# Infini-attention block with feed-forward: q and k projected as 32-column tiles straight from the raw weights, heads regrouped, new order of work

## The chip, the core and the metric

The kernel runs on one core of a Trainium2 chip. The metric is the device time of one execution in microseconds (us), lower is better. A time is given as the median of several runs; beside it there is one execution recorded by the hardware profiler, with its own time and its span (first to last recorded instruction).

The core has four computing engines that run side by side, each with its own instruction queue in program order: TensorE (PE; its weight loads are listed apart as PEld), VectorE (DVE), ScalarE (ACT) and GpSimd (POOL). SyncE (SP) issues the DMA transfers. Engines wait for each other on semaphores. All matmuls write to PSUM, which has 8 banks of 2 KB per partition; SBUF holds everything else.

## The reference, cut to what matters

One batch of 2048 tokens with 640 features, 32 heads of 20, bf16. The attention works on 4 segments of 512 tokens: causal softmax inside the segment, plus a compressive memory of all segments before.

```python
qs, ks, vs = q[:, :, s], k[:, :, s], v[:, :, s]          # from layernorm(x) @ wq, wk, wv
p = softmax(qs @ ks^T * scale + causal_mask)
a_dot = p @ vs
a_mem = (phi(qs) @ M) / (phi(qs) @ z + 1e-6)             # phi(t) = t + 1 if t > 0 else exp(t)
o = g * a_mem + (1 - g) * a_dot                          # g = sigmoid(beta), one per head
M = M + phi(ks)^T @ vs;  z = z + sum(phi(ks))            # carried to the next segment
...
h  = x + concat_heads(o) @ wo
h2 = h + silu(layernorm(h) @ w1) @ w2                    # 640 -> 1728 -> 640
```

## The kernel before, in words

**Layout.** The work of each segment is cut into 5 *chunks* of projected features (128 rows each) for q and for k, 8 *groups* of 4 heads, and 4 token blocks of 128. A group of heads sits in one tile of 128 partitions, one head in the first 20 rows of each quarter of 32 rows. Five such tiles (`QK`, `QK0` for segment 0) come straight from the projections and hold heads 0 to 19; the 12 rows that are free in each quarter carry pieces of heads 20 to 31 along. From these pieces 12 DMAs per segment (`virt`, line 897) put together the tiles `QKV` of groups 5 to 7.

**Weights of q and k.** The raw weights `wraw` lie, after their DMAs, in the room that `sT` has later. Since a chunk's 128 columns are not next to each other in them, `rearr` (lines 689 to 721) copies them into `wqr` and `wkr`: 12 tasks (`re_wq0`, `re_wq0h`, `re_wq1` to `re_wq4`, and the same for k), spread over VectorE, ScalarE and GpSimd by the order.

**A segment's front.** Layer norm of each block (`n1_st` statistics, `n1_rs` 1/sqrt on GpSimd, `n1_ap` apply); transposes to `tT` (in segment 0 five matmuls with the identity, `n1_tp`, and an eviction from PSUM, `n1_te`; in the others a DMA, `n1_tr`); projections `pr{s}{c}{w}` (w = 0 for q, 1 for k; five matmuls of 512 columns in two parts, `.0` and `.1`), evicted by `qe` (line 866 on ScalarE, 867 on VectorE); values `v` and their eviction `ve` (lines 832 and 833, into `Vx`, for segment 0 into a part of `sT`); phi by `ex` (exponential on ScalarE, line 873), `pa` and `pb` (VectorE). Chunk 0 of segment 0 is projected in halves of 256 tokens (`SPLIT0`, x and y).

**A group of heads** k = 8 s + g. Scores in quads of four row tiles, one head each (`qk{k}a`, `b`, `e`, matmuls at line 943 with `tile_position=(32*r, 0)`); exponentials `e{k}...` over two PSUM banks at once (line 964, 128x1024) or, where the order marks it `/W`, over four (line 960, 128x2048); causal masks `mk` on GpSimd; the product with V as four column tiles (`av`, line 999); its eviction times a gate (`oe`); then, back to tokens, `td` and from segment 1 on the memory part `tm`; normalisation `nm` on VectorE and `ad` on GpSimd. At a segment's end `kt`, `mz`, `ma`, `mb` update the memory, masked by `MzM`, which GpSimd makes at the start from the masks `mt`. The back of a segment is `ot`, `wo`, `rs`, `n2_...`, `h1` (matmuls), `th` (Tanh), `s`, `h2`, `o`, `out`.

**Forms of a matmul.** `mms` (line 547) emits either one matmul over the full array (line 550) or, where the order marks a task `/C`, four column tiles of 32 columns (line 551):

```python
    def mms(eng, out, lhsT, rhs, start, stop):

        if eng != "cols":
            return [lambda e: e.matmul(out, lhsT=lhsT, rhs=rhs, start=start, stop=stop)]
        return [lambda e, p=p: e.matmul(out[p:p + 32, :], lhsT=lhsT[:, p:p + 32], rhs=rhs, start=start, stop=stop,
                                        tile_position=(0, p)) for p in (0, 32, 64, 96)]
```

**What sets the order.** A table, `ORDER`, written out as text: 1439 entries in one sequence for all engines, each a task with, where there is a choice, its engine (`/A` ScalarE, `/D` VectorE, `/G` GpSimd, `/C` column tiles) and the slots of its buffers. `Graph.schedule` follows it and checks that predecessors come first; `Tracker` then adds the semaphore waits from what is read and written. So each engine's queue is fixed by the table. Entries `fillN` are N matmuls of 256 columns on a tile of zeros, `zpad` (line 622); nothing uses their result. There are 25 of them before the first transposes and 5 behind these. `zpad` is set to zero by VectorE (line 601), before the statistics of block 0. `warm` is a Tanh on ScalarE that reads `zpad` and writes two rows of `w2_sb`.

**Loads.** SyncE issues x blocks 0 and 1, blocks 2 and 3 together, wq and wk in two parts each, wv; the later loads (x4 on, wo, w1, w2) wait for the rearrangement of wk's first part.

## Time and profile before

| | |
|---|---|
| median of 3 runs | 296.78 us (296.61 to 297.32) |
| the profiled execution | 297.21 us, span 295.2 us |
| TensorE busy | 280.6 us (95%) |
| VectorE busy | 219.0 us (74%) |
| ScalarE busy | 216.5 us (73%) |
| GpSimd busy | 148.2 us (50%) |
| granted TensorE clock, mean | 1.0 |

A row of a timeline or chain gives start, length, engine, what is written, the line, and a count (x5) where several instructions are taken together; `out<-in` are the names of the tiles. A matmul's shape is contraction*output rows, then contraction x columns streamed. Matmuls are pipelined, so that one's listed length is longer than the time until the next one can start: durations here are taken from start to start of a run of many. A page's share of busy time is a mean over stages with different limits; the stages are read by stretches of the span.

### The profile page before, as it was taken

What the parts mean: (1) busy time and instruction counts of PE and PEld (TensorE: products, weight loads), DVE (VectorE), ACT (ScalarE), POOL (GpSimd) and SP (SyncE); (2) the same over time, 40 slices, a digit from 0 to 9 for tenths busy, and PEclk for the clock granted to TensorE, in tenths of its full rate; (3) what the DMA queues carried; (4) which work ended last, traced back from release to release, by engine and by line L of the source; (5) the groups of instructions that cost most, each with busy time, mean ns of one, the idle gap of its engine ahead of it and who ended that gap; (6) DMA issues with size and microseconds to landing.
All of it is one profiled execution on the core that took longest, in us unless ns stands there. A gap on an engine that the chain in (4) does not pass through costs nothing.

```text
span 295.2 us, 8471 instructions
## 1 busy us (share of the span) xinstructions
PE 280.6 (95%) x3537; PEld 158.1 (54%) x3561; DVE 219.0 (74%) x447; ACT 216.5 (73%) x263; POOL 148.2 (50%) x297
## 2 busy tenths in 40 slices
PE   7899889899999999999999999999999999999996
PEld 5554434536644545566643564556564657764574
DVE  4788899689999677999879867597655676734614
ACT  5799999799989999957899856979989641004500
POOL 4878777662777436946527552548464621300000
PEclk9999999999999999999999999999999999999999
DMA  7859349476530400442553312303221031330003
GB/s 223 288 151 232 57 115 229 96 235 90 87 66 18 104 4 3 75 100 46 81 135 101 77 27 53 58 2 54 62 69 47 2 67 26 67 91 0 0 2 111
DMA packets 48597, 24.72 MB, mean 84 GB/s; under 512 B 38896, under 2 KB 47472, under 8 KB 48560
## 3 DMA queue, kind: packets, MB, share of 16 engines
q1 hardware_dynamic: 48560, 24.19, 34.9%
q8 instruction: 28, 0.46, 0.6%
q14 instruction: 9, 0.07, 0.1%
HBM read 10.41 MB, written 2.62 MB: 44 GB/s over the span
## 4 chain that ended last, share of the span: by engine, by line
PE 64%; ACT 17%; DVE 10%; issue 3%; DMA 2%; POOL 2%; ACTq 0%; DVEq 0%
PE ps_all L550 47%; ACT PT L964 12%; PE ps_all L551 7%; PE ps_all L943 5%; PE ps_all L999 4%; DVE stt L754 3%; ACT PT L960 2%; DVE xn_rot L772 2%; DVE sT L1222 2%; DMA tT<-otok 2%; ACT th L1216 1%; ACT ex L873 1%; POOL PT L976 1%; DVE x_tok L1181 1%; PE ps_all L1117 1%
## 5 line engine op out<-in xcount | busy, mean ns | idle before, releaser
L964 ACT ACTIVATE PT<-ps_all 128x1024 bf16<-128x1024 f32 x114 | 109.3, 1035 | 15.5 <-PE ps_all L943 14.8
L976 POOL TENSOR_SCALAR_AFFINE_SELECT PT<-PT 128x512 bf16<-128x512 bf16 x128 | 82.0, 649 | 57.5 <-ACT PT L964 32.0
L1216 ACT ACTIVATE th<-ps_all 128x512 f32<-128x512 f32 (+1 forms) x56 | 31.5, 585 | 36.6 <-PE ps_all L550 27.8
L550 PE MATMUL ps_all<-w_sb,sT 128*128 128x320 bf16 x400 | 58.2, 299 | 0.1
L550 PE MATMUL ps_all<-tT,w_sb 128*128 128x512 bf16 x225 | 53.9, 379 | 1.3 <-issue 1.1
L1222 DVE SCALAR_TENSOR_TENSOR sT<-th,ps_all 128x512 bf16<-128x512 f32 (+1 forms) x56 | 36.2, 663 | 17.7 <-ACT th L1216 17.1
L550 PEld LDWEIGHTS ps_all<-w_sb,sT 128*128 128x128 bf16 x400 | 38.1, 98 | 16.6 <-issue 1.5
L960 ACT ACTIVATE PT<-ps_all 128x2048 bf16<-128x2048 f32 x23 | 43.2, 1879 | 3.4 <-PE ps_all L943 3.0
L550 PEld LDWEIGHTS ps_all<-tT,w_sb 128*128 128x128 bf16 x235 | 21.4, 98 | 25.0 <-issue 1.8
L754 DVE BATCH_NORM_STATS2 stt<-x_tok 128x6 f32<-128x320 bf16 x62 | 26.8, 473 | 1.3 <-DMA x_tok<-in_A_x_dram 1.2
L1259 DVE SCALAR_TENSOR_TENSOR x_tok<-ps_all,x_tok 128x640 bf16<-128x640 f32 (+1 forms) x17 | 13.2, 784 | 18.0 <-PE ps_all L550 17.1
L1077 POOL TENSOR_TENSOR otok<-on 128x320 bf16<-128x320 bf16 x24 | 19.2, 806 | 12.5 <-DVE on L1069 12.5
L867 DVE CAST QK<-ps_all 128x512 bf16<-128x512 f32 x26 | 17.9, 687 | 8.0 <-PE ps_all L550 6.5
L764 POOL TENSOR_TENSOR rst<-mvt,eps_c 128x1 f32<-128x1 f32 x32 | 7.0, 219 | 31.9 <-DVE mvt L757 30.0
L550 PE MATMUL ps_all<-tT,wkr 128*128 128x512 bf16 (+1 forms) x87 | 21.7, 368 | 1.0 <-issue 0.5
L772 DVE TENSOR_SCALAR xn_rot<-x_tok,mvt,rst 128x640 bf16<-128x640 bf16 x32 | 17.8, 564 | 4.3 <-POOL rst L766 3.8
L550 PE MATMUL ps_all<-tT,wqr 128*128 128x512 bf16 (+1 forms) x79 | 20.0, 367 | 1.0 <-issue 0.6
L1069 DVE TENSOR_TENSOR on<-ps_all,rd 128x640 bf16<-128x640 f32 x24 | 19.8, 824 | 0.8
L550 PE MATMUL ps_all<-wv_sb,tT 128*128 128x320 bf16 x130 | 19.7, 299 | 0.7 <-issue 0.7
L766 POOL TENSOR_TENSOR rst<-rst,eps_c 128x1 f32<-128x1 f32 x32 | 18.0, 563 | 2.5
L1015 DVE TENSOR_SCALAR oTs<-ps_all,lsc 128x512 bf16<-128x512 f32 x24 | 17.8, 742 | 0.8 <-PE ps_all L999 0.8
L999 PE MATMUL ps_all<-PT,Vx 128*32 128x512 bf16 (+3 forms) x384 | 17.3, 301 | 0.0
(113 smaller groups left out, 379.5 us busy)
## 6 DMA issues: line engine op xcount, KB each, us to landing
out_dram<-x_tok SPq DMA_DIRECT2D x15, 160.0 KB, 1.9
w_sb<-in_B_w_dram SPq DMA_DIRECT2D x5, 432.0 KB, 4.7
x_tok<-in_A_x_dram SPq DMA_DIRECT2D x3, 640.0 KB, 4.3
w_sb<-in_B_w_dram SPq DMA_DIRECT2D x3, 480.0 KB, 4.1
QKV<-QK SPq DMA_DIRECT2D x12, 72.0 KB
wv_sb<-in_A_wv_dram SPq DMA_DIRECT2D x1, 800.0 KB, 8.0
wo_sb<-in_A_wo_dram SPq DMA_DIRECT2D x1, 800.0 KB, 4.9
w_sb<-in_B_w_dram SPq DMA_DIRECT2D x1, 640.0 KB, 5.1
```

The lines of the kernel that those rows point to most:

```text
L550: return [lambda e: e.matmul(out, lhsT=lhsT, rhs=rhs, start=start, stop=stop)]
L551: return [lambda e, p=p: e.matmul(out[p:p + 32, :], lhsT=lhsT[:, p:p + 32], rhs=rhs, start=start, stop=stop, tile_position=(0, p)) for p i ...
L754: T.add(DV, lambda e, hh=hh: e.bn_stats(out=stt[:, s, 6 * hh:6 * hh + 6], in_=xb[:, 320 * hh:320 * hh + 320]), reads=R((xa, xsub)), writes ...
L772: T.add(eng, lambda e: e.tensor_scalar(out=xn_rot[:, xn.slot, :], in0=x_tok[:, b % 12, :], scalar1=mvt[:, s, 0:1], scalar2=rst[:, s, :], o ...
L960: T.add(AC, lambda e: e.activation(out=o, in_=src, func=ACT.Exp, scale=SCALE), reads=[("ps", z.slot + q) for z in (a, b) for q in range(2) ...
L964: T.add(AC, lambda e: e.activation(out=pt[:, pta.slot, q0:q0 + 2, 0:width], in_=sc3[:, b0:b0 + 2, 0:width], func=ACT.Exp, scale=SCALE), re ...
L976: fns.append(lambda e, v=v: e.affine_select(out=v, in_=v, pattern=[[0, 4], [1, 128]], compare_op=ALU.is_ge, fill=0.0, base=0, channel_mult ...
L999: fns.append(lambda e, j=j, r=r, h=h, pa=pa, pt=pt, co=co, q0=q0, ji=ji: e.matmul(bank(po)[32 * r:32 * r + 32, q0:hi], lhsT=vtile(vx)[:, j ...
L1069: T.add(DV, lambda e: e.tensor_tensor(out=on[:, ona.slot, :, :].rearrange("p b (x e) -> p b x e", e=DH), in0=v[:, :, :, 0:DH], in1=r2.unsq ...
L1077: T.add(PO, lambda e: e.tensor_tensor(out=o_dst, in0=on[:, ona.slot, 0, :].rearrange("p (i x) -> p i x", i=4), in1=on[:, ona.slot, 1, :].r ...
L1216: T.add(AC, lambda e: e.activation(out=th[:, tha.slot, lo:hi], in_=bank(ps)[:, lo:hi], func=ACT.Tanh, scale=0.5), reads=R((ps, [0])), writ ...
L1222: T.add(DV, lambda e: e.scalar_tensor_tensor(out=sT[:, f, lo:hi], in0=th[:, tha.slot, lo:hi], scalar=1.0, in1=bank(ps)[:, lo:hi], op0=ALU. ...
```

## The change

**Projections from raw weights.** `rearr`, `wqr` and `wkr` are gone; wq and wk are loaded as they are into `wq_sb` and `wk_sb`. Chunk c below 4 covers the columns 160c to 160c + 159, that is heads 8c to 8c + 7; its four column tiles take 32 columns each, 40 apart: an even head's 20 and the first 12 of the odd head behind it. So these matmuls always come as four column tiles. Chunk 4 holds the last 8 columns of all 16 odd heads; it is copied to `w4` by two tasks of four copies (`re_w4q`, `re_w4k`, both on GpSimd) and is projected in either form.

**Groups by parity.** Groups 0 to 3 are even heads straight from chunks 0 to 3; groups 4 to 7 are odd heads, put together in `QKV` (now four tiles) by 8 DMAs per segment instead of 12. The heads of a group are now two apart, so `otok`, the gate and the masks are addressed with other strides. The masks are three types and a selector `tsel` instead of four types, and lie in `th` while they are needed; the zeros of the warm-up lie in `on`.

**Segment 0 in pieces.** All chunks of segment 0 are projected in pieces into one bank: q in four pieces of 128 tokens (a to d), k in two of 256. One eviction of 512 columns follows; before, chunk 0 had two of 256.

**Waits of the loads.** The later loads no longer wait for a rearrangement.

**Order.** The table is written anew, 1500 entries. The warm-up matmuls come as `fill1` and `fill2` between other entries, 40 in all: 30 before the first transposes, 6 behind these, 3 and 1 later. `warm` stands behind the transposes of block 2, statistics of blocks 1 and 3 go to ScalarE (before: block 1), no entry has `/W`.

```diff
-MZB = [0, 2, 4, 6, 9]
-MZN = [2, 2, 2, 3, 3]
-GRP_BLK = [[(0, 0)], [(1, 2)], [(2, 4)], [(3, 6)], [(4, 9)],
-           [(0, 1), (3, 7)], [(1, 3), (4, 10)], [(2, 5), (3, 8), (4, 11)]]
+MZB = [0, 2, 4, 6, 8]
+MZN = [2, 2, 2, 2, 4]
+GRP_BLK = [[(g, 2 * g)] if g < 4 else [(g - 4, 2 * (g - 4) + 1), (4, 4 + g)] for g in range(NG)]
+HEADS = [(8 * (g % 4) + g // 4, 2) for g in range(NG)]
-SPLIT0 = ((0, 0), (0, 1))
+PIECES0 = ([(0, 1), (1, 2), (2, 3), (3, 4)], [(0, 2), (2, 4)])
...
 ORDER = """
-epsc:0 mt0 halfc x0:8 x1:9 x2:0,1 w_q0:0 w_q1 w_k0 w_k1 w_wv:0 n1_st1/A:2,2 mta0 mt3 iota sel zpad warm:0 n1_st0:0
+iota:0 halfc x0:0 epsc n1_st0:2,1 mt0:0 mta0 mt1 zpad:1 fill1:0 fill2:1 sel fill2:2 fill1:3 mtb0 fill1:4 mt2 mta2
...
     def mms(eng, out, lhsT, rhs, start, stop):
-        if eng != "cols":
+        if eng != "cols" and len(lhsT.shape) == 2:
             return [lambda e: e.matmul(out, lhsT=lhsT, rhs=rhs, start=start, stop=stop)]
-        return [lambda e, p=p: e.matmul(out[p:p + 32, :], lhsT=lhsT[:, p:p + 32], rhs=rhs, start=start, stop=stop,
+        quad = (lambda p: lhsT[:, p // 32]) if len(lhsT.shape) > 2 else (lambda p: lhsT[:, p:p + 32])
+        return [lambda e, p=p: e.matmul(out[p:p + 32, :], lhsT=quad(p), rhs=rhs, start=start, stop=stop,
                                         tile_position=(0, p)) for p in (0, 32, 64, 96)]
+    def chunk(w, kc, c):
+        if c < 4:
+            return (wq_sb, wk_sb)[w][:, kc, 160 * c:160 * c + 160].rearrange("p (r e) -> p r e", e=40)[:, :, 0:32]
+        return w4[:, w, kc, :]
...
-        dma("w_" + k, [(W["wk"], [0])] if kind == "plain" else [], wr, lambda e: e.dma_start(out=dst, in_=src), ...)
+        dma("w_" + k, [], wr, lambda e: e.dma_start(out=dst, in_=src), ...)
...
-                for hh, (b0, b1) in enumerate([(0, 2), (2, 4)] if s == 0 and (c, w) in SPLIT0 else [(0, 4)]):
-                    ps = G.alloc("ps", 1)
+                ps = G.alloc("ps", 1)
+                for hh, (b0, b1) in enumerate([(0, 4)] if s else PIECES0[w]):
...
-                            fns = [f for kc in ks for f in mms(eng, bank(ps)[:, lo:hi], wt[:, kc, c, :],
-                                                               tT[:, xTa.slot, kc, lo:hi], kc == 0, kc == NC - 1)]
+                            fns = [f for kc in ks for f in mms(eng, bank(ps)[:, lo:hi], chunk(w, kc, c),
+                                                               tT[:, xTa.slot, kc, lo:hi], kc + hh == 0, kc == NC - 1 and end)]
...
-            virt(3 * r, allq((0, 1, 2)), QKV[p:p + 12, :, :, :], qkt[p + 20:p + 32, 0:3, :, :])
-            virt(3 * r + 1, allq((3, 4)), QKV[p + 12:p + 20, 0:2, :, :], qkt[p + 20:p + 28, 3:5, :, :])
-            virt(3 * r + 2, allq((3, 4)), QKV[p + 12:p + 20, 2, :, :], qkt[p + 28:p + 32, 3:5, :, :])
+            virt(2 * r, allq((0, 1, 2, 3)), QKV[p:p + 12, :, :, :], qkt[p + 20:p + 32, 0:4, :, :])
+            virt(2 * r + 1, allq((4,)), QKV[p + 12:p + 20, :, :, :], qkt[p:p + 32, 4, :, :])
...
-                        h = 4 * g + r
+                        h = HEADS[g][0] + HEADS[g][1] * r
```

391 lines of the change are left out of this document (194 added, 197 removed).

## Prediction

> **What bounds the kernel now.** I read the busy time by stretch first, then the chain of waits, then the order of time on single engines at the places that the change touches. The first view gives, for each stretch in us, the busy time of PE, PEld, DVE, ACT and POOL with instruction counts, then the clock, the DMA share and GB/s.
>
> ```profile
> 13.50:51.70 38.20, 35.19 (x388) 16.44 (x391) 33.22 (x79) 38.11 (x46) 29.88 (x75) 1.00 0.65 164
> 51.70:84.00 32.30, 30.07 (x508) 16.66 (x512) 27.87 (x56) 29.34 (x33) 20.34 (x40) 1.00 0.57 125
> 84.00:234.00 150.00, 147.06 (x2170) 81.31 (x2183) 117.03 (x232) 127.48 (x146) 84.14 (x140) 1.00 0.27 56
> 234.00:295.20 61.20, 58.28 (x405) 36.51 (x407) 32.13 (x58) 12.65 (x23) 4.71 (x10) 1.00 0.17 44
> ```
>
> Three regimes follow each other. From 13.5 to 51.7 ScalarE is busy 38.11 of 38.20 us: the softmax exponentials of segment 0 set the pace. From 51.7 to 84 no engine is full, and VectorE, TensorE and ScalarE take turns. From 84 on TensorE has 147.06 of 150 and then 58.28 of 61.2: what is left is matmul work, and a start that is later or earlier is carried to the end. So three things count: when the first exponential starts, how much ScalarE has to do until segment 0 is through, and how much TensorE work remains then.
>
> The chain of waits shows how the first exponential comes about, and what ScalarE does behind it (start, length, what).
>
> ```profile
> 0.81 2.41 DMA x_tok<-in_A_x_dram
> ...
> 9.35 0.45 DVE xn_rot L772
> 9.79 0.40 DVE tT L791
> ...
> 10.44 0.73 DVE wkr L713 x2
> ...
> 11.22 1.83 PE ps_all L550 x15
> ...
> 13.07 0.39 ACT w_sb L866
> ...
> 13.48 0.63 ACT ex L873
> 14.11 1.88 ACT PT L964 x2
> ...
> 17.94 1.77 ACT PT L960
> 19.71 0.35 ACT w_sb L866
> ...
> 20.06 0.25 ACT bsel L648
> 20.32 0.12 ACT zf L659
> 20.43 0.60 ACT sT L832
> 21.03 0.48 ACT w_sb L866
> 21.51 0.60 ACT sT L832
> 22.11 1.03 ACT ex L873 x2
> ...
> 31.52 5.39 ACT PT L964 x6
> ...
> 48.13 0.51 ACT ex L873
> ```
>
> Before the first exponential (14.05 us on ScalarE's own row) stand the load of x, the layer norm, the transposes, 0.73 us of weight rearrangement on VectorE, the projections and an eviction. Behind it ScalarE goes from exponential to exponential at 5.39/6 = 0.90 us each, with other work between. Group 8's first score tile, the first of segment 1, starts at 57.34 us and is where this phase ends:
>
> ```profile
> 57.34 0.39 PE L943 MATMUL ps_all<-QK 20*128 20x512 bf16 x4
> ```
>
> **The projections as column tiles.** Four tiles of 32 columns run side by side. The trace of before has the two forms of the same projection, in order of time on TensorE: L551 in column tiles, L550 over the full array.
>
> ```profile
> 58.65 0.65 PE ps_all L551 x12
> ...
> 62.10 1.18 PE ps_all L550 x5
> ...
> 198.07 1.09 PE ps_all L999 x32
> ```
>
> ```profile
> 63.23 0.39 PE L943 MATMUL ps_all<-QK 20*128 20x512 bf16 x4
> 63.56 0.61 PE L550 MATMUL ps_all<-tT,wkr 128*128 128x512 bf16 x2
> ```
>
> Twelve tile matmuls are three sets of four: 0.65/3 = 0.217 us for 512 columns. Five full matmuls take 1.18; less 0.10 for a change of form (below), that is 0.216 each. So the form costs nothing by itself. The pieces of 128 columns are new only for projections: the 32 matmuls at 198.07 are two products with V, 2 x 1280 columns with every eighth set 128 wide or more, in 1.09 us, which is 0.426 ns per column. So 128-column sets take about 0.057 us. A change of form (full, column, row) costs about 0.10 us: the four row tiles of 512 columns at 63.23 are followed by full matmuls 0.33 later, 0.216 of it their columns. Counted over the order TensorE makes 180 before and 176 after. Its columns apart from the warm-up matmuls are the same (254.4 before, 254.3 us after). Value for TensorE over the whole run: -0.4 us; bounds -0.6 and +0.4, the lower if every switch saved counts, the upper if each of the 92 sets of 84 columns that go over to column form costs about 0.004 us.
>
> The Trainium skill, TensorEngine Tiling, section Restrictions and Gotchas, says that column tiling rules out fast weight load; a rival below gives what that could do.
>
> **The start.** The change removes 12 rearrangements, of which 0.73 us stood on the chain, and lets q be computed per token block. But VectorE's order changes as well. The rows are VectorE's first instructions, before and then after; zpad is the tile of zeros which the warm-up matmuls read (after, it lies in the tile `on`).
>
> ```order
> L644 TENSOR_SCALAR ident<-iot 128x128
> L601 MEMSET zpad 128x128
> L754 BN_STATS stt<-x_tok 128x6 x2
> L757 BN_AGGR mvt<-stt 128x2
> L772 TENSOR_SCALAR xn_rot<-x_tok,mvt,rst 128x640
> ```
>
> ```order
> L757 BN_STATS stt<-x_tok 128x6 x2
> L760 BN_AGGR mvt<-stt 128x2
> L614 MEMSET on 128x128
> L657 TENSOR_SCALAR ident<-iot 128x128
> L693 TENSOR_REDUCE tsel<-ident 128x4
> L775 TENSOR_SCALAR xn_rot<-x_tok,mvt,rst 128x640
> ```
>
> The zeros moved from before the statistics of block 0, which wait for x, to behind them. TensorE's first instructions, before and after (ident with xn_rot are the transposes of x):
>
> ```order
> L622 MATMUL ps_all<-zpad 128x256 x25
> L781 MATMUL ps_all<-ident,xn_rot 128x128 x5
> L622 MATMUL ps_all<-zpad 128x256 x5
> L781 MATMUL ps_all<-ident,xn_rot 128x128 x15
> L550 MATMUL ps_all<-tT,wqr 128x256 x5
> ```
>
> ```order
> L635 MATMUL ps_all<-on 128x256 x30
> L784 MATMUL ps_all<-ident,xn_rot 128x128 x5
> L635 MATMUL ps_all<-on 128x256 x6
> L784 MATMUL ps_all<-ident,xn_rot 128x128 x5
> L635 MATMUL ps_all<-on 128x256 x3
> L555 MATMUL ps_all<-tT,wq_sb 32x128 x60
> ```
>
> The first transpose now stands behind 30 warm-up matmuls instead of 25, and these start later. What they cost, in order of time on TensorE, VectorE and in two stretches of the warm-up alone:
>
> ```profile
> 1.92 0.17 DVE L601 MEMSET zpad<- 128x128 uint32 x1
> ...
> 2.14 5.16 PE L622 MATMUL ps_all<-zpad 128*128 128x256 bf16 x25 [2.14 <-DVE zpad L601]
> 7.13 0.44 PE L781 MATMUL ps_all<-ident,xn_rot 128*128 128x128 bf16 x5
> ...
> 2.14:4.27 2.13, 2.13 (x11) 1.00 0.89 257
> ...
> 3.24 0.89 DVE L754 BATCH_NORM_STATS2 stt<-x_tok 128x6 f32<-128x320 bf16 x2 [1.16 <-DMA x_tok<-in_A_x_dram]
> 4.16 0.21 DVE L757 BATCH_NORM_AGGREGATE mvt<-stt 128x2 f32<-128x12 f32 x1
> ...
> 9.71 0.82 DVE L791 CAST tT<-ps_all 128x640 bf16<-128x640 f32 x1
> ```
>
> The stretch of 2.13 us holds ten of them and the edge of an eleventh: 0.213 us for 256 columns. In full work 512 columns take 0.216, so these run at half speed. All 25 took 7.13 - 2.14 = 4.99 us; with 0.213 slow and 0.108 fast that is 22 slow ones and 3 fast: TensorE came to speed some 4.6 us after its first matmul. After the change the zeros are written behind the aggregate, at 4.16 + 0.21 + 0.17, so the first warm-up starts at about 4.55. With the same 4.6 us, 22 slow and 8 fast make 5.55 us: the first transpose comes at 10.1 instead of 7.13. Bounds: all 30 fast, 7.8; all slow, 10.9.
>
> The Trainium skill, TensorE: Matmul & The Clock Gate, Part 1, says that the clock is halved by default and opens after about 3.4 us of sustained work, counted in a window that runs freely; the trace shows the two speeds and 4.6 us. By 3.4 us the first transpose would be at 9.5, and the total 0.6 us less than the sum below.
>
> From there, with the durations of before: the eviction on VectorE starts 0.48 behind (0.44 and a semaphore) and takes 0.82, to 11.4; blocks 2 and 3 are normalised only behind it on VectorE (two of 0.45), to 12.3. TensorE has six more warm-ups, the second transposes and three warm-ups by 11.65, then ten q sets of 0.057 and, when block 1 is evicted, five more, to 12.6; the last two transposes by 13.3; k over blocks 0 and 1 (eight of 0.108) by 14.3, q of block 2, k over blocks 2 and 3 (five of 0.108) by 15.1, q of block 3 by 15.4. Then q's eviction (0.2 to start, 0.48), ex (0.52) and the first exponential at about **16.7**, against 14.05: **+2.65 us**. Bounds: with all warm-ups fast the arrival of wk holds k back, and it is about 14.3, +0.2; with all slow, +3.5. I take the value by the speed that the trace shows.
>
> **ScalarE until group 8.** Its rows behind the first exponential, before and after:
>
> ```order
> L964 ACTIVATE PT<-ps_all 128x1024 x4
> L960 ACTIVATE PT<-ps_all 128x2048
> L866 ACTIVATE w_sb<-ps_all 128x512
> L648 ACTIVATE bsel<-beta_bc 128x32
> L659 ACTIVATE zf<-beta_bc 128x32
> L832 ACTIVATE sT<-ps_all 128x32x20
> L866 ACTIVATE w_sb<-ps_all 128x512
> L832 ACTIVATE sT<-ps_all 128x32x20
> L873 ACTIVATE ex<-w_sb 128x512 x2
> ```
>
> ```order
> L966 ACTIVATE PT<-ps_all 128x1024 x2
> L869 ACTIVATE w_sb<-ps_all 128x512
> L966 ACTIVATE PT<-ps_all 128x1024 x2
> L869 ACTIVATE w_sb<-ps_all 128x512
> L966 ACTIVATE PT<-ps_all 128x1024 x2
> L876 ACTIVATE ex<-w_sb 128x512
> L966 ACTIVATE PT<-ps_all 128x1024 x2
> ```
>
> The two v evictions (sT) have gone to VectorE (0.60 each), bsel and zf to before the first exponential (0.24 together), and one ex of segment 1 to behind group 8 (0.51). Two double exponentials of 1.77 are now four of 0.90, +0.07. Together 1.20 + 0.24 + 0.51 - 0.07: **-1.88 us**. The 40 exponentials of segment 0 stay.
>
> **Behind group 8.** VectorE pays: the phi work of segment 1 and two v evictions slide past group 8, net about 1.1 us more between groups 8 and 12.
>
> ```profile
> 68.00:84.00 16.00, 15.27 (x212) 9.04 (x206) 15.40 (x31) 14.61 (x17) 10.73 (x22) 1.00 0.54 86
> ```
>
> There VectorE is busy 15.40 of 16.00, so up to all of it counts; over the 32.3 us of 51.7 to 84 it has 4.4 us free, so it may be none. I take **+0.4**, bounds 0 and 1.1. From group 8 to the end TensorE has 229.2 us left, before 229.4: **-0.14** (its other 0.26 lie earlier, beside ScalarE).
>
> Fewer QKV copies (8 instead of 12 per segment), new strides of `otok`, masks from `tsel` and the two small rearrangements on POOL lie beside other work, POOL being busy 29.88 of 38.20; if that cover is gone, the two rearrangements are about 2.5 us of POOL early on.
>
> Sum: 2.65 - 1.88 + 0.40 - 0.14 = **+1.03 us**. The profiled execution took 297.21 with a span of 295.2; that becomes about 298.2, and from the median of the runs, 296.78, which is 0.43 lower, **297.8 us**. What a measurement of this kernel can tell from no change is about 0.3%, 0.9 us.
>
> **Rivals.** *The start is not late* (0.30). If TensorE is fast almost at once, or the transposes are not held, the first exponential stays near 14.3 and ScalarE's 1.88 us come through: 296.78 + 0.2 - 1.88 - 0.14 + 0.4 = 295.4; with VectorE's 0.4 hidden and TensorE's full 0.6 gained, 294.5. For it: 0.73 us of rearrangement are off the chain. Against it: 25 warm-ups took 4.99 us. It decides from a first transpose before about 8 us.
>
> *VectorE becomes the bound of segment 0* (0.20). Between the first exponential and the scores of group 4 the order has some 22.3 us of VectorE work against 21.2 on ScalarE; before it was 18.7 against 22.5. Then the phase gives back 1.1 us, groups 8 to 12 the full 1.1, and the clock comes late too (3.5 at the start instead of 2.65): 297.8 + 1.1 + 0.7 + 0.85 = 300.4. For it: 33.22 of 38.20 already; against it: the early VectorE work is statistics of the next blocks, which nobody waits for at once.
>
> *Weights of column tiles load one by one* (0.03). One weight load of 32 columns shows 96 ns in the groups of instructions:
>
> ```profile
> L551 PEld LDWEIGHTS ps_all<-tT,w_sb 128*32 128x32 bf16 x100 | 2.4, 96 | 2.0 <-issue 0.4 <-DVE sT L1222 0.2
> ```
>
> Four in series would be 0.38 us against 0.216, on 120 sets of 512 columns in segments 1 to 3: +20 us, 318. The 0.65 us for twelve speak against it. This is the case in which the tiling page's rule would bite.
>
> **How the numbers follow.** The sum as it stands has 0.47, between 296.4 and 299.2: a clock that opens up to 1 us earlier in the warm-up and VectorE's 0.4 hidden make the lower end, the 3.5 at the start and most of VectorE's 1.1 the upper. Range: 294.5, the first rival's end, to 300.4, the second's. Faster by over 0.3% (below 295.9) is most of the first rival: 0.25. Within 0.3% (up to 297.7) are the lower half of the sum's own case and the rest of the first rival: 0.28. Slower, the other half and the two other rivals: 0.47.
>
> **What the profile after would show.** Right: the first warm-up near 4.5 us, the first transpose near 10, the first exponential near 16.7, group 8's first scores near 58.1. Wrong: an exponential before 15, or a group 8 that is later than 59 with ScalarE idle in between (then VectorE's queue or TensorE's bound the phase), or a first column-tile set of 512 columns above 0.25 us.

## The result, and the profile after

The changed kernel takes 311.13 us (median of 4 runs, 310.44 to 312.89), the kernel before 296.87 beside it: a ratio of 1.0488, 95% interval 1.0438 to 1.0537. It is 14.3 us slower; the forecast was 1.0. The profiled execution took 311.75 us, with a span of 310.0 and a mean granted clock of 0.983 (before 297.21, 295.2 and 1.0). Executions of the changed kernel and its variants scatter by 1 to 2%; every ratio leaves out those more than 1.5% above the fastest of their kernel, which the medians in us do not, and the one that is profiled may lie at the upper end.

TensorE, ScalarE and the places where the forecast put marks, in order of time (of after; one fence for each engine):

```profile
4.47 6.37 PE L635 MATMUL ps_all<-on 128*128 128x256 bf16 x30 [4.47 <-DVE on L614]
...
10.68 0.44 PE L784 MATMUL ps_all<-ident,xn_rot 128*128 128x128 bf16 x5
...
16.95 0.39 PE L945 MATMUL ps_all<-w_sb 20*128 20x512 bf16 x4
...
47.13 0.61 PE L945 MATMUL ps_all<-QKV 20*128 20x512 bf16 x4 [5.12 <-DMA QKV<-w_sb]
```

```profile
17.40 1.94 ACT L966 ACTIVATE PT<-ps_all 128x1024 bf16<-128x1024 f32 x2
```

The start is close to the forecast: first warm-up at 4.47 us (4.55 was said), first transposes 10.68 (10.1), first exponential 17.40 (16.7), so 3.35 us later than before where 2.65 was said. Then comes something that the forecast has not: at group 4 TensorE stands for 5.12 us until `QKV` lands. Group 8's first scores start at 67.44 instead of 57.34 us, where 58.1 had been expected.

The same stretches as shown of before, for after (PE, PEld, DVE, ACT, POOL busy with counts, clock, DMA share, GB/s):

```profile
13.50:51.70 38.20, 30.45 (x752) 20.10 (x753) 27.67 (x65) 28.92 (x34) 24.55 (x61) 0.91 0.85 178
51.70:84.00 32.30, 31.41 (x643) 15.56 (x636) 26.17 (x55) 30.42 (x36) 19.30 (x33) 1.00 0.56 102
84.00:234.00 150.00, 144.67 (x2707) 81.24 (x2709) 113.63 (x233) 126.60 (x162) 80.36 (x134) 0.99 0.38 61
```

In the first stretch ScalarE is busy 28.92 of 38.20 us, before it was 38.11: no engine is full now. The clock is 0.91 and the DMA share 0.85 (1.00 and 0.65 before). Around the wait, finer:

```profile
38.00:47.00 9.00, 3.14 (x69) 1.69 (x69) 6.65 (x16) 4.48 (x5) 4.70 (x10) 0.87 0.81 99
47.00:52.00 5.00, 4.87 (x42) 2.21 (x42) 0.78 (x2) 3.88 (x4) 0.64 (x1) 0.56 1.53 307
```

After 5 us without work TensorE has a mean granted clock of 0.56 from 47 to 52. So the wait is paid twice: while it lasts, and then in 5 us of work at about half speed.

Why is the gather late? SyncE's queue, first of before, then of after (start, length of the issuing):

```profile
29.85 6.70 SPq L898 DMA_DIRECT2D QKV<-w_sb  x9
36.59 1.21 SPq L796 DMA_TRANSPOSE tT<-xn_rot  x1
```

```profile
26.17 2.67 SPq L599 DMA_DIRECT2D w_sb<-in_B_w_dram  x3
30.14 0.57 SPq L599 DMA_DIRECT2D w_sb<-in_B_w_dram  x1
34.38 6.90 SPq L901 DMA_DIRECT2D QKV<-w_sb  x8
41.32 0.45 SPq L599 DMA_DIRECT2D wo_sb<-in_A_wo_dram  x1
43.77 2.27 SPq L799 DMA_TRANSPOSE tT<-xn_rot  x1
```

The main part of the gather starts 4.5 us later (before, three of its twelve copies go out even earlier, at 21.54 and 26.48), and its last part is under way from 40.61 for 6.42 us in the chain of waits. Three loads of w1 and one of w2, issued between 26.17 and 30.71, stand ahead of it in the queue. But its data are late too: VectorE evicts the last chunk that it needs from 35.47 to 36.75, before from 30.18 to 30.87. And it is needed a group earlier: by the old grouping groups 5 to 7 read `QKV`, by parity groups 4 to 7 do. After it wo is loaded, and the last DMA transpose of segment 1's four token blocks is issued at 43.77 instead of 36.59.

Group 12, the first of segment 1 that reads `QKV`, does not wait for the gather. In order of time in SyncE's queue, on VectorE and on TensorE, after:

```profile
81.24 6.32 SPq L901 DMA_DIRECT2D QKV<-QK  x8
87.60 1.23 SPq L799 DMA_TRANSPOSE tT<-xn_rot  x1
...
92.97 0.45 DVE L775 TENSOR_SCALAR xn_rot<-x_tok,mvt,rst 128x640 bf16<-128x640 bf16 x1 [1.86 <-DMA tT<-xn_rot]
...
95.21 0.40 PE L945 MATMUL ps_all<-QKV 20*128 20x512 bf16 x4 [1.92 <-DVE oTs L1017]
```

TensorE waits 1.92 us for VectorE, and VectorE had waited 1.86 us for a transpose that SyncE issued right behind the eight copies of the gather.

A ledger, an estimate of the time that TensorE loses (idle, or slow at a low clock: length of a stretch less its columns at full speed), after minus before, between the first scores of successive groups, places about 15 us: start 2.25; groups 0 to 3, 2.5; from group 3 to 4, 5.5; 4 to 8, 0.15; 8 to 13, 2.8; 13 to 22, 0.4; 22 to 23, 1.2; the rest 0.5. Most of it lies before group 13.

One more kind of stop has no counterpart in the forecast. In order of time on TensorE, after:

```profile
24.82 0.39 PE L945 MATMUL ps_all<-w_sb 20*128 20x512 bf16 x2
25.87 0.39 PE L945 MATMUL ps_all<-w_sb 20*128 20x512 bf16 x2 [0.66 <-issue]
```

Four row tiles of one task are torn apart after the second, by 0.66 us, with nothing that they wait for. Counting all that the trace has in TensorE's queue from the start of the program (matmuls, weight loads and semaphore instructions), this stop comes at a count that leaves 193 when divided by 256. So do the two others in after (0.38 us at 19.2, 0.27 at 29.6), and nearly all of 0.2 us or more in the runs below (193 to 195); the exception is one of 0.3 to 0.5 us near 150 us in before and three of its variants. The page of after and of before list the fetching of instructions as a queue of its own (packets, MB, share of 16 engines):

```profile
q8 instruction: 39, 0.64, 0.9%
```

```profile
q8 instruction: 28, 0.46, 0.6%
```

0.64 MB in 39 packets is 16 KB each. With one matmul for each weight load (some matmul records are missing) and 118 and 110 semaphore instructions and the like, TensorE's queue has 9972 entries after and 7232 before: 39.0 and 28.3 times 256. In all 20 profiles the number of these packets is that of the boundaries in TensorE's queue: the packets are its instructions by 256. The trace has the times of the packets as well. Of 40 stops at such a boundary 39 end 1.3 to 1.8 us after a packet has landed; the stop above ends at 25.87, the packet had come at 24.38. So TensorE stops because its next instructions are late. Column tiles take eight instructions where the full array takes two, and q in pieces of 128 tokens takes four times as many again. The Trainium skill, Runtime: NRT & Kernel Launch, section Instruction fetch mechanics, has instructions come in blocks of 16 KiB, 256 of them, over a DMA queue, and the cost of crossing a block "mostly hidden". The count agrees (39 packets, 39.0 times 256). In this execution the three stops come to 1.3 us, so most of the 39 boundaries are hidden; in the runs below single stops are longer.

### The profile page after: what moved, and what is told of

Read it like the earlier page. It is cut to its first block, busy times and chain, and to the rows that moved or that the text cites. A ratio compares the mean times of both kernels' runs of the same rounds, so it can differ in the third digit from the quotient of the medians.

```text
span 310.0 us, 11215 instructions
## 1 busy us (share of the span) xinstructions
PE 288.7 (93%) x4916; PEld 168.2 (54%) x4927; DVE 213.9 (69%) x438; ACT 217.7 (70%) x283; POOL 147.4 (48%) x287
## 4 chain that ended last, share of the span: by engine, by line
PE 70%; DMA 9%; DVE 9%; ACT 7%; issue 2%; SPq 1%; POOL 0%; DVEq 0%; ACTq 0%
PE ps_all L553 37%; PE ps_all L555 19%; ACT PT L966 7%; PE ps_all L945 6%; PE ps_all L1001 4%; DMA tT<-xn_rot 3%; DMA x_tok<-in_A_x_dram 3%; PE ps_all L635 2%; DMA QKV<-w_sb 2%; DMA phiKt<-phiK 1%; DVE stt L757 1%; DVE oTs L1017 1%; DVE xn_rot L775 1%; PE ps_all L1119 1%; DVE phiK L883 1%
## 5 line engine op out<-in xcount | busy, mean ns | idle before, releaser
L966 ACT ACTIVATE PT<-ps_all 128x1024 bf16<-128x1024 f32 x160 | 154.3, 1026 | 27.4 <-PE ps_all L945 26.5
L553 PEld LDWEIGHTS ps_all<-w_sb,sT 128*128 128x128 bf16 x416 | 39.6, 98 | 17.3 <-issue 1.5
L553 PE MATMUL ps_all<-tT,w_sb 128*128 128x512 bf16 x145 | 33.8, 379 | 1.0 <-issue 0.6
L555 PE MATMUL ps_all<-tT,w_sb 128*32 128x512 bf16 x420 | 26.3, 380 | 0.1
L945 PE MATMUL ps_all<-QKV 20*128 20x512 bf16 (+3 forms) x256 | 16.3, 308 | 8.6 <-DMA QKV<-w_sb 5.1
L553 PEld LDWEIGHTS ps_all<-tT,w_sb 128*128 128x128 bf16 x155 | 14.4, 98 | 16.3 <-issue 0.9
L555 PE MATMUL ps_all<-tT,wq_sb 128*32 128x128 bf16 (+1 forms) x560 | 22.1, 288 | 1.0 <-DMA tT<-xn_rot 0.4
L555 PE MATMUL ps_all<-tT,wk_sb 128*32 128x512 bf16 (+1 forms) x400 | 22.2, 350 | 0.3 <-issue 0.3
L1017 DVE TENSOR_SCALAR oTs<-ps_all,lsc 128x512 bf16<-128x512 f32 x26 | 19.2, 744 | 2.4 <-PE ps_all L1001 2.3
L775 DVE TENSOR_SCALAR xn_rot<-x_tok,mvt,rst 128x640 bf16<-128x640 bf16 x32 | 15.6, 493 | 4.4 <-POOL rst L769 2.2
L945 PEld LDWEIGHTS ps_all<-QKV 20*128 20x128 bf16 x256 | 4.7, 92 | 22.0 <-issue 12.5
```

What stands on the lines that cost most here:

```text
L555: return [lambda e, p=p: e.matmul(out[p:p + 32, :], lhsT=quad(p), rhs=rhs, start=start, stop=stop, tile_position=(0, p)) for p in (0, 32, ...
L945: fns.append(lambda e, j=j, o=o, r=r, q0=q0, q1=q1, qa=qa, ka=ka: e.matmul(ps_all[:, o:o + q1 - q0], lhsT=ka[32 * r:32 * r + DH, 128 * j:1 ...
L966: T.add(AC, lambda e: e.activation(out=pt[:, pta.slot, q0:q0 + 2, 0:width], in_=sc3[:, b0:b0 + 2, 0:width], func=ACT.Exp, scale=SCALE), re ...
L1017: f = lambda e: e.tensor_scalar(out=o, in0=i_, scalar1=lsc[:, g:g + 1], scalar2=None, op0=ALU.mult)
```

## The experiments

The theory: **(1)** the wait for the gather, a group earlier and behind loads, with the half clock behind it; **(2)** the late start, as forecast. Rivals: **(3)** the column tiles themselves, by their form or by their number of instructions; **(4)** the later loads in SyncE's queue and on the DMA engines. All kernels of a comparison ran beside the kernel before on the same chip; medians are of 6 runs (5 for the fourth).

### First: each suspect alone

**No wait for the gather**, in after:

```diff
-            return (qv, list(range(8))), QKV[:, g - 4, 0, :], QKV[:, g - 4, 1, :]
+            return (W["wv"], [0]), wv_sb[:, 0, 0:L], wv_sb[:, 1, 0:L]
```

> The changed kernel, but the scores of groups 4 to 7 read two constant slices of wv instead of the gathered tiles QKV (so the odd heads' attention is left out); the 8 gather DMAs per segment are still issued, nobody waits for them before the end. Gather theory (the added time is mostly TensorE waiting for QKV, with the clock that drops in the wait): group 4's first scores come near 41.5 us instead of 47.1, the 5.3 us gap before them is gone, the clock stays at 1.0 between 47 and 52, and the total falls by 7 to 10 us, to 301 to 304. Column-tile theory (the cost is spread over all projections): less than 1 us is saved. Load theory (freed loads and transposes collide on the DMA queues): some gaps before QKV go, but VectorE still waits for the transposes at 88 to 93 us, and 3 to 6 us are saved.

Measured: 312.03 us, 1.0525 (1.0494 to 1.0556). It gains nothing. On TensorE the wait has gone from group 4, and another stands behind group 4 (of this kernel):

```profile
51.88 2.32 PE L555 MATMUL ps_all<-tT,wq_sb 128*32 128x512 bf16 x20 [2.67 <-DMA tT<-xn_rot]
```

Segment 1's first projection waits 2.67 us for a DMA transpose, which SyncE issues at 45.66, behind the gather, wo, kt02 and w1. Theory 1, as the wait alone, falls: it hid a second one behind it. The profiled execution (312.71 us) also has a stop of 2.00 us at a boundary, at 19.15, where after has one of 0.38.

**Loads of w1 and wo later**, in after:

```diff
 ORDER = """
...
-ve01/D w_w1_3 w_w1_2 pr030b.1
+ve01/D pr030b.1
...
-pa011:1 w_w1_1 n1_ap7:3
+pa011:1 n1_ap7:3
...
-e3a0:1 w_wo:0 pb021 kt02:2 w_w1_0 e3a2
+e3a0:1 pb021 kt02:2 e3a2
...
-e5a2:3 pb031
+e5a2:3 w_w1_3 w_w1_2 w_w1_1 w_wo:0 w_w1_0 pb031
```

> The changed kernel with five weight loads (w1 rows 0 to 3 and wo) issued by SyncE behind the scores of group 5 instead of between 26 and 43 us, that is behind the gather. Load theory: the gather lands 3 us or more earlier, group 4 starts before 44.5 us and the total falls by 3 to 6 us. Gather theory in its pure form (the gather is late because it is issued late and is long by itself): group 4 stays within 1 us of 47.1 and the total within 1 us of 311.

Measured: 314.42, 1.0604 (1.0576 to 1.0632): slower. On TensorE, of this kernel:

```profile
43.64 0.40 PE L946 MATMUL ps_all<-QKV 20*128 20x512 bf16 x4 [2.35 <-DMA QKV<-w_sb]
...
70.28 0.33 PE L1120 MATMUL ps_all<-sT,phiKt 128*32 128x42 bf16 x16 [5.42 <-DMA phiKt<-phiK]
```

The wait at group 4 fell from 5.12 to 2.35 us and group 8 starts at 63.70 (67.44 after), but the five loads now lie ahead of segment 0's memory update kt03, for which TensorE stands 5.42 us from 64.9. The same bytes have been put in another's way. The gather itself is issued at 33.13 here, only 1.25 us earlier than in after, so of the 4.5 us by which it starts late the loads in the queue explain 1.25. Its last copy, issued at 38.95, is there within 4.7 us instead of 6.42: the loads also slowed the transfer.

**Zeros first**, in after:

```diff
 ORDER = """
...
-n1_st0:2,1 mt0:0 mta0 mt1 zpad:1 fill1:0
+zpad:1 n1_st0:2,1 mt0:0 mta0 mt1 fill1:0
```

> The changed kernel with the zeros of the warm-up written before the statistics of block 0 on VectorE, as in the kernel before. All theories have the first warm-up near 2.2 us and the first scores 2 to 2.5 us earlier. If the chain to the gather starts with the projections, the whole kernel gains 2 to 2.5 us (about 308.8); if the weights' arrival or SyncE sets the gather, group 4 stays at 46 to 47 us and less than 1 us is gained.

Measured: 312.51 (309.20 to 315.13), 1.0494 (1.0453 to 1.0536): no gain. The first scores come at 15.81 instead of 16.95, behind a stop of 2.14 us at a boundary. Then, in order of time on TensorE and by stretches of this kernel (profiled at 315.13 us):

```profile
17.52 0.56 PE L556 MATMUL ps_all<-tT,wq_sb 128*32 128x128 bf16 x26
22.48 0.72 PE L556 MATMUL ps_all<-tT,wq_sb 128*32 128x128 bf16 x18 [4.41 <-issue]
```

```profile
18.00:20.00 2.00, 0.08 (x6) 0.00 (x0) 0.44 (x1) 0.68 (x2) 1.75 (x9) 1.00 1.08 382
20.00:22.40 2.40, 0.00 (x0) 0.00 (x0) 0.00 (x0) 0.00 (x0) 0.00 (x0) 0.79 0.27 98
22.40:25.00 2.60, 2.52 (x62) 1.69 (x65) 0.22 (x1) 1.20 (x2) 0.00 (x0) 0.50 0.03 6
```

In the middle of a task of column tiles TensorE stops for 4.41 us, at about instruction 705 = 2 x 256 + 193; all engines fall silent, DMA is at 382 GB/s when it begins, and the clock is 0.50 behind it. The packet of instructions starts at 20.13, when the loads of wv and x end, and lands at 21.20; TensorE goes on at 22.48. The 4.41 us are those of one execution; that an earlier start gains nothing is what all of them say.

**Column tiles in the kernel before**: every `pr` entry of its table marked `/C`.

```diff
 ORDER = """
...
-pr100.0:4 pr100.1
+pr100.0/C:4 pr100.1/C
```

> The kernel before, with every projection of q and k as four column tiles (from the rearranged weights), nothing else changed. Column-tile theory (weights of column tiles load one by one, or four small matmuls cost more than one): 5 us or more above 296.9. My reading of the trace (0.220 against 0.216 us for a set of 512 columns): within 0.9 us of 296.9.

Measured: 301.38, 1.0157 (1.0135 to 1.0178), +4.6 us. An estimate of its parts from the trace: a set of 512 columns takes 0.219 us on average against 0.216 (0.5 us over some 160 sets); its order makes 22 more changes of form, at 0.10 about 2.2; its stops at boundaries are 1.75 us before 57.30 and 0.67 before 174.40, against one of 0.69 in before (1.7 more). That is 4.4 of 4.6. So the form is dear in an order that was not made for it, but half of that is changes of form, which after has fewer of (176 against 180); the part from the number of instructions is the 1.7.

### Second: pairs, and the terms in the other kernel

**The five loads behind kt03**, in after (shown against the loads later, above):

```diff
-e5a2:3 w_w1_3 w_w1_2 w_w1_1 w_wo:0 w_w1_0 pb031
+e5a2:3 pb031
...
-kt03:4 pr110.0:7
+kt03:4 w_wo:0 w_w1_0 w_w1_1 w_w1_2 w_w1_3 pr110.0:7
```

> The changed kernel with the five weight loads (w1 rows 0 to 3, wo) issued by SyncE behind the last key transposes of segment 0 (kt03, some 60 us) instead of between 26 and 43 us. Load theory (SyncE's queue and the DMA engines are too full around the gather): group 4 starts at 43 to 44 us as in the run with the loads behind group 5, the 5.6 us stall at 64.7 of that run is gone since the transposes no longer stand behind the loads, and the total is 306 to 308.5. If the transfers do not matter and TensorE's own instruction stream does, the total stays within 1 us of 311.

Measured: 308.20 (306.01 to 311.04), 1.0386 (1.0349 to 1.0423): 2.9 us less than after, the intervals apart. The loads' place is worth that much. Its profiled execution took 311.04 us, with a stop of 3.31 us at 18.47, so that the gain cannot be followed in it.

**q in halves of 256 tokens**, in after (two pieces a chunk instead of four, half the instructions of segment 0's q; the order is the same but for these pieces, the first of which start later):

```diff
-PIECES0 = ([(0, 1), (1, 2), (2, 3), (3, 4)], [(0, 2), (2, 4)])
+PIECES0 = ([(0, 2), (2, 4)], [(0, 2), (2, 4)])
```

> The changed kernel with segment 0's q in two pieces of 256 tokens instead of four of 128: the same columns in 160 fewer column-tile matmuls and as many fewer weight loads, but the first pieces start later. Instruction theory (TensorE stops every 256 instructions until the next 16 KB of them are there, while the DMA engines are full): the stops at 19.0, 24.8 and 29.3 us (1.8 us in all) become one or two shorter ones, group 3 starts 1 to 2.5 us earlier, and the total falls by 1 to 3 us. If the count of instructions does not matter: group 3 within 0.5 us of 37.95, and the total within 1 us of 311.

Measured: 309.81, 1.0456 (1.0419 to 1.0493): overlaps with after, inconclusive alone.

**Zeros late in the kernel before**: `zpad` and `warm` behind `n1_st0`, 30 and 6 warm-ups.

```diff
-zpad warm:0 n1_st0:0
+n1_st0:0 zpad warm:0
...
-fill25
+fill30:3
...
-fill5
+fill6:2
```

> The kernel before with the zeros of the warm-up behind the statistics of block 0 and 30 + 6 warm-up matmuls, as in the changed kernel. Start theory, as predicted: first warm-up at 4.5, first exponential 2.0 to 2.7 us later, the total 2.0 to 2.7 us above 296.9. If the start is not on the path: within 0.9 us of 296.9.

Measured: 299.13, 1.0075 (1.0046 to 1.0104), +2.2 us. Its first scores come at 14.80 (13.61 before); in this kernel the rearrangement stays on the chain and blocks 2 and 3 aren't moved. The start is 1.2 us later and the whole 2.2 (1.4 to 3.1): in the kernel before a late start is not absorbed, as the forecast had it. Why the end is later than the start by another 1 us is not shown.

**One wait of after in the kernel before**: segment 0's group 4, which needs nothing from the gather there, waits for it.

```diff
+                if s == 0 and g == 4 and (qv, list(range(12))) not in ra:
+                    ra.append((qv, list(range(12))))
```

> The kernel before with one dependency more: the scores of group 4 in segment 0 also wait for the gather (QKV), which there only group 5 and later need. Gather theory: TensorE waits 2 to 4 us more before group 4 (which started at 36.45; the last gather is issued at 35.9) and the total rises by 2 us or more. If the gather is hidden by other work at that place: group 4 within 1 us of 36.5 and the total within 0.9 us of 296.9.

Measured: 299.77 (297.95 to 302.35), 1.0119 (1.0082 to 1.0155), +3.2 us. The wait is 1.92 us (its row names no releaser), and the stretches behind it show the second half of the price, in the profiled execution (302.35 us):

```profile
38.76 0.62 PE L945 MATMUL ps_all<-w_sb 20*128 20x512 bf16 x4 [1.92 <-issue]
```

```profile
36.00:39.00 3.00, 1.08 (x24) 0.53 (x22) 2.74 (x6) 1.46 (x2) 2.37 (x6) 0.87 0.43 82
39.00:42.00 3.00, 3.00 (x14) 1.34 (x10) 0.36 (x2) 1.94 (x2) 1.09 (x3) 0.50 0.63 164
42.00:45.00 3.00, 2.97 (x38) 1.16 (x38) 1.84 (x4) 2.24 (x3) 0.43 (x3) 0.50 0.00 0
45.00:48.00 3.00, 3.00 (x10) 0.69 (x9) 2.73 (x8) 2.70 (x4) 2.77 (x8) 0.50 0.51 51
48.00:51.00 3.00, 3.00 (x22) 0.97 (x20) 1.61 (x4) 2.59 (x3) 2.85 (x9) 0.92 0.54 148
```

TensorE is busy from 39 on, at a clock of 0.50 for nine microseconds. Other executions pay less: the mean granted clock is 0.983 here, 0.994 in four others and 1.00 in the one of 297.95 us. In before, with its 147.06 of 150 us busy later on, this is not given back.

### Third: both waits away, and filling the wait

**40 warm-up matmuls into the wait**, in after:

```diff
-w_w2_1 qk4a0:2,6
+w_w2_1 fill40:0 qk4a0:2,6
```

> The changed kernel with 40 more warm-up matmuls (4.4 us of TensorE) just ahead of group 4's first scores, where TensorE otherwise waits 5.3 us for the gather and then runs at a granted clock of 0.56 until 52 us. Clock theory: the wait stays (group 4 at 46.5 to 48 us), the clock stays near 1.0 from 47 to 52, and the total falls by 1 to 2 us. If the slow clock there lies beside other waits: the total stays within 0.9 us of 311.

Measured: 309.65, 1.0442 (1.0411 to 1.0474); 1.5 us less than after, but the intervals overlap. The clock did what was expected, by stretches:

```profile
38.00:47.00 9.00, 7.40 (x123) 4.93 (x123) 8.27 (x19) 6.05 (x7) 5.32 (x10) 1.00 0.70 103
47.00:52.00 5.00, 4.65 (x58) 2.91 (x55) 0.62 (x1) 2.92 (x4) 1.18 (x2) 1.00 1.25 243
```

**No gather wait and loads behind kt03**: the edits of the first and the fifth run together.

```diff
-            return (qv, list(range(8))), QKV[:, g - 4, 0, :], QKV[:, g - 4, 1, :]
+            return (W["wv"], [0]), wv_sb[:, 0, 0:L], wv_sb[:, 1, 0:L]
...
-kt03:4 pr110.0:7
+kt03:4 w_wo:0 w_w1_0 w_w1_1 w_w1_2 w_w1_3 pr110.0:7
```

> The changed kernel with the loads moved to the end of segment 0's transfers, and groups 4 to 7 reading two slices of wv instead of the gathered tiles (so the odd heads' attention is left out; the gather is issued, nobody waits for it). Queue theory (without the gather's wait TensorE waited for the transposes of segment 1, which SyncE issues behind gather and loads): with both out of the way group 4 starts near 41.5, no gap over 1.5 us is left between 38 and 55 us, and the total is 4 us or more below the run without the wait alone (312.0), at 303 to 308. If the wait for the gather were the whole cost, this run would be no better than the loads alone (308.2).

Measured: 304.72, 1.0279 (1.0249 to 1.0308): 7.3 us less than without the wait alone, 3.5 less than with the loads moved alone. With both, the first stretch looks like this:

```profile
13.50:51.70 38.20, 32.79 (x837) 21.00 (x838) 32.92 (x74) 32.70 (x39) 25.90 (x64) 1.00 0.74 119
```

Clock 1.00, and the engines have more to do. Once the loads are out of the way the wait for the gather is worth 3.5 us, alone it was worth nothing. Together the two give 6.4 of the 14.3 us. What they leave, some 8 us, has other causes: group 4 still starts at 43.64 here (36.45 before), of which 2.95 us are the start and 2.1 are three stops at boundaries.

**Repair** (loads behind kt03, q in halves, 20 warm-ups into the wait), without and with the zeros first:

```diff
-PIECES0 = ([(0, 1), (1, 2), (2, 3), (3, 4)], [(0, 2), (2, 4)])
+PIECES0 = ([(0, 2), (2, 4)], [(0, 2), (2, 4)])
...
-w_w2_1 qk4a0:2,6
+w_w2_1 fill20:0 qk4a0:2,6
...
-kt03:4 pr110.0:7
+kt03:4 w_wo:0 w_w1_0 w_w1_1 w_w1_2 w_w1_3 pr110.0:7
```

> The changed kernel with three repairs at once: the five loads at the end of segment 0's transfers, q of segment 0 in two pieces of 256, and 20 warm-up matmuls ahead of group 4's scores. If the three costs add up (2.9 for the loads, 1.3 for the pieces, 1 for the clock): 305 to 307. If they are one and the same wait seen thrice: 308 or more.

> The same three repairs and the zeros of the warm-up written first. If the late start is a cost of its own (2.2 us in the kernel before): 1.5 to 2.5 us below the three repairs alone. If the earlier start only runs into the stops at the 256-instruction blocks, as in the run with the zeros first alone: within 1 us of the three repairs, with stops of 2 us or more before 25 us.

Measured: 308.17, 1.0387 (1.0346 to 1.0429), and 308.27, 1.0363 (1.0321 to 1.0405): the gains don't add, and the earlier start (first exponential at 14.19 instead of 17.82) again gives nothing. The second has a stop of 1.04 us at 21.3 that the first has not. In order of time on TensorE, the first of the two:

```profile
64.60 0.72 PE L1001 MATMUL ps_all<-PT,sT 128*32 128x512 bf16 x14
...
67.89 0.23 PE L1001 MATMUL ps_all<-PT,sT 128*32 128x128 bf16 x2 [2.58 <-issue]
```

```profile
65.00:68.00 3.00, 0.42 (x13) 0.14 (x4) 0.28 (x1) 0.86 (x1) 2.83 (x6) 1.00 0.94 375
68.00:71.00 3.00, 3.00 (x42) 1.37 (x44) 1.50 (x2) 1.94 (x2) 1.16 (x3) 0.58 0.06 18
```

The loads, put together here, take 375 GB/s, and a fetch that falls among them stops TensorE in the middle of a product with V (its packet starts at 65.60, lands at 66.61, and TensorE goes on at 67.89); the clock is 0.58 behind it.

### Fourth: loads spread out, and the whole sum in the kernel before

**The five loads one by one, issued by ScalarE** (behind e7a2, e8a0, e8e2, e9b2, e10a0): alone, with halves and 20 warm-ups, and with the zeros first as well.

```diff
-e3a0:1 w_wo:0 pb021 kt02:2 w_w1_0 e3a2
+e3a0:1 pb021 kt02:2 e3a2
...
-e7a2 qk7b0:0,4
+e7a2 w_wo/A:0 qk7b0:0,4
...
-e8a0 mk8a
+e8a0 w_w1_0/A mk8a
```

> The changed kernel with the five weight loads (wo, w1 rows 0 to 3) issued one at a time by ScalarE, at exponentials of groups 7 to 10 (58 to 80 us), instead of by SyncE between 26 and 43 us. If what the loads cost is their place around the gather and a full DMA queue when the next instructions are due: 2.5 to 4.5 us below 311.1, no stop over 1 us at a 256-instruction block between 55 and 85 us. If loads only move the cost: above 309.5.

> The loads spread as in the run before, q of segment 0 in two pieces, 20 warm-up matmuls ahead of group 4. The three repairs with the loads in one block kept group 8 at 63.5 us but stopped for 2.7 us at 65.1 with the clock at 0.58 behind it. If that stop came from the block of loads: it is gone, group 9 starts near 70 instead of 74.8, and the total is 303 to 305.5. If it came from something else: 308.

> The same with the zeros of the warm-up written first: 1 to 2.5 us less than the run before, 301 to 304, so still 4 us or more above the kernel before (the gather that group 4 waits for, and the waits of segments 1 to 3, are still there).

Measured: 311.17, 1.0453 (1.0416 to 1.0490); 307.09, 1.0325 (1.0293 to 1.0357); 308.28, 1.0370 (1.0326 to 1.0413). Spread alone, the loads gain 1 us by the ratio, within the intervals. The second is the best full kernel with the change, and still 10 us above before; the third's earlier start gives nothing again. Where the gain is lost shows in the first scores of groups (us; profiled at 297.21, 311.75, 311.05, 309.02 and 309.49):

| group | before | after | second | third | no gather wait, spread |
|---|---|---|---|---|---|
| 0 | 13.61 | 16.95 | 16.88 | 13.95 | 13.77 |
| 4 | 36.45 | 47.13 | 43.78 | 42.76 | 39.47 |
| 8 | 57.34 | 67.44 | 62.87 | 61.95 | 59.97 |
| 12 | 83.23 | 95.21 | 95.67 | 94.86 | 92.78 |

The variants are 5 to 7 us ahead at group 8 and nearly level with after at group 12. From one to the other they take 32.8 to 32.9 us (after 27.8, the run without the wait and with the loads behind kt03 27.6). Each of the three has a stop at the same boundary there, of 2.94, 2.93 and 2.85 us, with half the clock for 3.4 us behind it; together that is about 4.6 us (an estimate: 2.9 and half of 3.4), of the size of the 5 us by which they take longer.

**No gather wait with spread loads, halves and zeros first**, without warm-ups in the wait (the last column):

```diff
-            return (qv, list(range(8))), QKV[:, g - 4, 0, :], QKV[:, g - 4, 1, :]
+            return (W["wv"], [0]), wv_sb[:, 0, 0:L], wv_sb[:, 1, 0:L]
...
-PIECES0 = ([(0, 1), (1, 2), (2, 3), (3, 4)], [(0, 2), (2, 4)])
+PIECES0 = ([(0, 2), (2, 4)], [(0, 2), (2, 4)])
...
-n1_st0:2,1 mt0:0 mta0 mt1 zpad:1 fill1:0
+zpad:1 n1_st0:2,1 mt0:0 mta0 mt1 fill1:0
...
-e7a2 qk7b0:0,4
+e7a2 w_wo/A:0 qk7b0:0,4
```

> The changed kernel without the wait for the gather (groups 4 to 7 read two slices of wv, so the odd heads' attention is left out), with the loads spread, q in two pieces and the zeros first, without extra warm-up matmuls. If gather, loads and start explain the cost: 298 to 302, with group 12 before 90 us. If group 12 stays near 94 us as in every run so far, something other than the gather sets it, and the total is 304 or more.

Measured: 307.19 (303.99 to 309.49), 1.0327 (1.0283 to 1.0371). Without any wait for the gather in group 12 it still comes there at 92.78. In order of time on TensorE:

```profile
87.28 0.34 PE L945 MATMUL ps_all<-QK 20*128 20x384 bf16 x4
90.48 0.24 PE L945 MATMUL ps_all<-QK 20*128 20x128 bf16 x4 [2.85 <-issue]
```

A fetch stop of 2.85 us, at about instruction 3008 = 11 x 256 + 192. Its packet starts at 87.98, 4.4 us after the boundary ahead was passed at 83.62, while segment 1's gather and segment 2's transposes move; from 91 to 95 the clock is 0.62.

**All three waits in the kernel before** (groups 4, 12 and 20 wait for the gather):

```diff
+                if s < 3 and g == 4 and (qv, list(range(12))) not in ra:
+                    ra.append((qv, list(range(12))))
```

> The kernel before with the one dependency more in segments 0, 1 and 2: the scores of the fifth group of each (4, 12, 20) also wait for the gather. Gather theory: the 3.2 us of segment 0 alone, and 2 to 3 us more in segment 1, where the last gather is issued at 83.7 and group 12 started at 83.2; 4.5 to 6.5 us above 296.5. If only segment 0 is short of time: 3 to 4 us above.

Measured: 309.48, 1.0429 (1.0396 to 1.0463), +12.9 us, with waits of 2.10, 3.53 and 3.59 us, 9.2 in all. The other 3.7 us go with slow work behind them; the second wait and its stretches (profiled at 311.21 us):

```profile
90.38 0.62 PE L945 MATMUL ps_all<-QK 20*128 20x512 bf16 x4 [3.53 <-DMA QKV<-QK]
```

```profile
90.00:93.00 3.00, 2.40 (x15) 1.28 (x17) 1.22 (x3) 1.94 (x2) 0.00 (x0) 0.50 0.19 44
93.00:96.00 3.00, 3.00 (x15) 1.31 (x13) 1.68 (x5) 1.11 (x2) 0.71 (x2) 0.50 0.02 5
96.00:99.00 3.00, 3.00 (x34) 1.27 (x34) 2.37 (x4) 2.64 (x4) 1.78 (x3) 1.00 0.01 3
```

**Waits, late zeros and column tiles, all in the kernel before**: the edits of three runs above together.

```diff
+                if s < 3 and g == 4 and (qv, list(range(12))) not in ra:
...
-zpad warm:0 n1_st0:0
+n1_st0:0 zpad warm:0
...
-pr100.0:4 pr100.1
+pr100.0/C:4 pr100.1/C
```

> The kernel before with three things of the changed kernel put in: the zeros late with 30 + 6 warm-up matmuls (2.2 us alone), all projections of q and k in column tiles (4.6 us alone), and the fifth group of segments 0 to 2 waiting for the gather (3.2 us or more). If these make up the change and add: 306 to 309. If they hide behind each other: 303 or less, and most of the change's cost lies elsewhere, in its order of loads and transfers.

Measured: 319.04, 1.0720 (1.0679 to 1.0760), +22.5 us, where the three alone sum to 2.2 + 12.9 + 4.6 = 19.7. So in the order of before these three cost more than after's 14.3. They are no account of the 14.3, since after's own order covers part of them: it waits for the gather at group 4 only, at group 12 for VectorE (above) and at group 20 not at all. With the one wait of segment 0 the three alone would sum to 2.2 + 3.2 + 4.6 = 10.0.

## Why the prediction was wrong

**The step that failed** is "Fewer QKV copies (8 instead of 12 per segment) ... lie beside other work", priced at nothing. The copies are fewer, but by the parity grouping they are due a group earlier, and most of them are issued 4.5 us later. The diff says the first (`HEADS`, groups 4 to 7 in `QKV` instead of 5 to 7), SyncE's queue the second; the forecast asked what the copies cost and not when they must have landed. TensorE waits 5.12 us for them at group 4, and that stretch has 5.5 us of the ledger. Put into the kernel before, this due time costs 3.2 us in segment 0. (The 12.9 for three segments are no cost of after, which waits for the gather once.) That is shown; but it is not the gather alone: taking its wait away gave nothing until the loads were moved as well (304.72 together, so 6.4 of the 14.3 us). The gather costs once more behind group 8: it holds SyncE's queue from 81.24 to 87.56, the transpose behind it is late for VectorE, and group 12 waits 1.92 us, part of the 2.8 between groups 8 and 13. What that is worth no run shows.

**The place of the loads** was not priced. The new table puts three loads of w1 close ahead of the gather, wo and a fourth behind it, and the last transpose of segment 1 comes 7 us later. The removed waits did not do this: in before the rearrangement of wk's first part ends at 11.2 us, long ahead of these places. Moved alone: -2.9 us, shown.

**The start** was right in kind: 17.40 against 16.7 for the first exponential, so +3.35 where +2.65 was forecast and +3.5 was the bound; +2.2 us for the part of it that was put into the kernel before. But an early start gives nothing back in the changed kernel: with zeros first and the first exponential at 14.19 and 14.40 the two repaired kernels stayed at 308.3, where the first rival had 295.4. Stops at boundaries of 1.0 and 1.3 us near 22 us take part of it; the rest of the loss is not traced.

**ScalarE's -1.88 us** did not come through. It presupposed that ScalarE paces segment 0; it is busy 28.92 of 38.20 us there. The term of +0.4 on VectorE behind group 8 was work; at group 12 what holds VectorE is a wait for a transpose. And **"a start that is later or earlier is carried to the end"** held for the start of before, not for gains in after: 5 us at group 8 were gone at group 12.

**The column tiles** were judged by their columns: 0.217 us a set, "the form costs nothing by itself". In after a set of 512 columns takes 0.219, within the bounds. What was missing is their number. 2,740 more TensorE instructions are 11 more fetches (39 packets against 28), and a fetch that comes late stops TensorE: 1.3 us in all in after's profile, 0.8 to 6.6 in its variants'. How much of the 14.3 us this is cannot be given as one number. Half the q instructions gave 1.3 us, not distinguishable from none.

**The rivals.** VectorE was not the bound of segment 0 (27.67 of 38.20 busy), weights of column tiles do not load one by one (0.219 us a set, not 0.38), and the start was late. All cases of the forecast shared the assumption that the phase is paced by an engine's work, so its range could not hold a wait.

**Open**: the 8 us that stay without the gather's wait and with the loads moved. Start and stops are part of them; a full account was not made. Group 12 starts at 90 to 99 us in every variant, against 83.23: in after behind a late transpose, in three variants behind a fetch stop. Whether it is the gather, which moves in packets of 8 KB at 0.99 us each after and of 6 KB at 0.71 before, or the transposes that delays that fetch was not separated. No version with the change came near the kernel before.

## What to carry to other kernels

When data are regrouped, don't only count the copies: write down for each when its first reader is due now, and what stands ahead of it in the queue that issues it. A wait on the pacing engine is to be priced with the slow clock behind it, and here one wait taken away showed the next, so two suspects in one queue are tried alone and together. Count instructions as well as columns before splitting matmuls into tiles, above all where loads keep the DMA engines busy.
